# A seven-tap convolution and a SwiGLU feed-forward block on one core: four head-taps change engine in the lead-in, and some words of pair 1's list change place

## The chip, the cores and the metric

The kernel runs on one core of a Trainium2 chip. A core has a matrix engine (TensorE, PE in the profile), a vector engine (VectorE, DVE), a scalar engine (ScalarE, ACT), a general engine (GpSimd, POOL) and an engine that issues DMAs (SyncE, SP). Each works through its own list of instructions in order, and semaphores tie the lists together. The metric is the device time of one execution in microseconds (us). The kernel before took 2473.61, 2478.57 and 2479.82 us in three runs; the median is 2478.57.

## The reference

```python
def _attn_ref(x, weight):                 # x: 8 x 4096 x 192, weight: 8 heads x 7 taps
    w = softmax(weight, axis=-1)          # 7 weights for each head of 24 channels
    x_pad = six rows of zeros in front of each sequence
    out[b, s, h, g] = sum over k of w[h, k] * x_pad[b, s + k, h, g]

def _moe_ref(x, w_gate, w_val, w_out, rms_g):      # x: 32768 x 192 tokens
    xn = x / sqrt(mean(x * x) + 1e-06) * rms_g
    g = xn @ w_gate                       # 192 x 1536
    val = xn @ w_val                      # 192 x 1536
    return (g * sigmoid(g) * val) @ w_out # 1536 x 192
```

The convolution runs along the sequence, one weight for each of 8 heads and 7 taps; its output goes token by token through an RMS norm and a SwiGLU block in float32. The weight matrices come in float64 and are turned into float32 on the chip.

## The kernel before, in words

The 32768 tokens are cut into 32 pairs of 1024 tokens, and a pair into two groups of 512. Pair 0 and pair 1 are special, pairs 2 to 31 repeat one list of words.

Lead-in (pair 0). `conv_first` makes the convolution of pair 0 with the 8 x 7 head-taps shared between two ways. VectorE multiplies and adds the taps `mine`, (1, 3, 5, 6), straight into the tile `y`, one instruction for each head (L418, L422). ScalarE multiplies the others into the tiles `kept` (L404), and TensorE adds them up in the four PSUM banks `ps[0]` to `ps[3]` by multiplying with a unit matrix (L408): four matmuls (one per bank, each recorded as two) for each group of heads. Of the last tap in `mine`, 6, the first `share` = 2 heads also go this second way. Then L428 adds each bank into its part of `y`, in the order 0, 1, 2, 3; after bank 1 and after bank 3, `heat` sends matmuls whose results nobody reads (one after bank 1, three after bank 3), into a second bank of the tile that holds `ps[3]`. `cross` follows: ScalarE squares rows 0 to 5 of `y` (L544; bank c holds rows 2c and 2c+1), VectorE rows 6 and 7 (L551, L554), L558 begins the norm's factors, and TensorE turns `y` round (L589). The weights are converted meanwhile (`convert`, L305 to L345), and `plain` runs pair 0's products (L1091).

Pair 1 has its own hand-written list, `FIRST`; the pairs after it run through `ORDER`. A list is a sequence of words that are emitted in order, and each engine keeps that order among its own instructions. `p3` lets TensorE do three more pieces of the pair's products; `W` advances the preparation of the product weights (`prepare`: L754, L757, L761, L763, L767, L769, then a store to `wd`, L773); other words name an engine (V, A, G, S) and an act. A `+` means the next pair, `++` the one after that, `-` the one before.

The output matmul of a pair is done with seven products instead of eight (a Strassen form). Per chunk j of the hidden features there are four cells a, b, c, d:

- `Aga.j`: ScalarE takes silu of cell a's gate half (L987). `Vma.j`: VectorE multiplies it with the value half into the tile `ht` (L994), which also frees the PSUM tile of that cell for another product (L882 in pair 1, L910 later).
- `Vh1.j`, `Vh3.j`, `Vh2.j`, `Vh4.j`: sums and differences of the four cells, written back in place (L964).
- steps `o1.j` to `o7.j`: TensorE multiplies one of these with a part of the output weights (L937, 12 recorded matmuls in a step). `o7.5` needs `Vh3.5`, `o6.5` needs `Vh2.5`, the steps `o3` need `Vh4`.
- `Ac1`, `As7`, `Ac2`: ScalarE copies of accumulators (L675). `VC21`, `VC22`: VectorE adds them (L1011); `VC21` frees the accumulator tile that the next pair's first product takes, and `VC22` must be done before the steps `o3`, which write the same accumulator.

Words for the pairs ahead: `Vcv5` is tap 5 of the convolution (L445; tap 0 on ScalarE is L441), `Asq`, `Vred`, `Gpow`, `Vbc`, `Gmul` the norm (`Gmul` is POOL's L495), `Spl.i` and `Sft.i` send the tokens out and fetch them back turned, `Sld.i` loads head i of the tokens of a later pair (L154), and `An.g`, `Vd.g`, `Gl.g` or `Vl.g` split operand g of the next pair into the three parts that the products use (`An` L675, `Vd` L820, `Gl` and `Vl` L818). `R` starts the ring: ten loads of prepared weights (L790, 192 KB each) into a tile that the tokens of pair 2 have held until then, so that `R` waits for the last reader of those tokens, `Vd.0`. The products of pair 2 begin with `P5.0` and `P1.0` (L910), the first two words of `ORDER`, ahead of `VC22` and the last six steps `o3` of pair 1.

Of the kernel before, what the change touches and what calls it, by code (L numbers as in the profile page):

```python
# [14 lines left out]
ALU = mybir.AluOpType  # L15
# [5 lines left out]
def kernel(  # L21
# [10 lines left out]
    nc = tc.nc  # L32
# [3 lines left out]
    H, K = weight.shape  # L36
    GS = D // H
# [8 lines left out]
    NJ = PT // P  # L46
# [47 lines left out]
    )  # L94
    FIRST = (
# [14 lines left out]
    )  # L110
    LINE = (
# [56 lines left out]
    def load(p):  # L168
# [34 lines left out]
        out=ps[6][:, 0 : H * K], lhsT=ones[:], rhs=w_row[:], start=True, stop=True,  # L203
# [24 lines left out]
    def load_in(u, q):  # L228
        cols = slice(u * NF * P, (u + 1) * NF * P)
        t = big.tile([P, 2, NF, T], F32, name="ht")  # L230
        t = t[:].rearrange("p a f t -> p (a f t)")[:, 0 : KP * NF * P * 2].bitcast(U32)
        t = raw["in", u] = t.rearrange("p (k n two) -> p k n two", k=KP, two=2)
        if u == 0:
            hold(t[:, :, 0, 0].bitcast(F32))
        for w, rows, turn in ((moe_w_gate, LOW, 0), (moe_w_val, UPP, 1)):
            for k in range(KP):
                at = (k + turn) % KP * HP
                q.dma_start(out=t[rows, k], in_=words(w)[at : at + HP, cols, :])
# [13 lines left out]
    hs = work.tile([P, NP, T], F32, name="hs")  # L252
# [4 lines left out]
    def load_out(i):  # L257
# [19 lines left out]
    taps = cst.tile([P, H, K], F32, name="taps")  # L277
    nc.vector.tensor_reduce(out=stat[:, :, 0], in_=w_sb, axis=AX.X, op=ALU.max)
    nc.vector.tensor_tensor(
        out=taps[:], in0=w_sb, in1=stat[:].to_broadcast([P, H, K]), op=ALU.subtract  # L280
# [7 lines left out]
        out=taps[:], in0=taps[:], in1=ssum[:].to_broadcast([P, H, K]), op=ALU.mult  # L288
# [98 lines left out]

    ys = {}

    def conv_first(mine, share):  # L390

        t = x_sb.pop(0)
        y = ys[0] = yp.tile([P, NJ, D], F32, name="y")
        theirs = [k for k in range(K) if k not in mine]
        two = NJ // 4
        for i, k in enumerate([theirs[0], mine[-1]] + theirs[1:]):
            xk, m = t[:, k : k + NJ, :], next(kept)
            cuts = (0, share) if k in mine else (0, H // 2, H)
            if k == theirs[-1]:
                cuts = (0, H // 2, H // 2 + 2, H)  # L400
            for lo, hi in zip(cuts, cuts[1:]):
                for h in range(lo, hi):
                    hs = slice(h * GS, (h + 1) * GS)
                    nc.scalar.mul(m[:, :, hs], xk[:, :, hs], taps[:, h, k : k + 1])  # L404
                part = slice(lo * GS, hi * GS)
                for c in range(4):
                    to = ps[c][:, 0 : two * D].rearrange("p (j d) -> p j d", d=D)
                    nc.tensor.matmul(  # L408
                        out=to[:, :, part], lhsT=unity, rhs=m[:, c * two : (c + 1) * two, part],
                        start=(i == 0 and lo == 0), stop=True, skip_group_check=True,  # L410
                    )
        for k in mine:
            xk = t[:, k : k + NJ, :]
            for h in range(share if k == mine[-1] else 0, H):
                hs = slice(h * GS, (h + 1) * GS)
                w = taps[:, h, k : k + 1]
                if k == mine[0]:
                    nc.vector.tensor_scalar(  # L418
                        out=y[:, :, hs], in0=xk[:, :, hs], scalar1=w, scalar2=None, op0=ALU.mult
                    )  # L420
                else:
                    nc.vector.scalar_tensor_tensor(  # L422
                        out=y[:, :, hs], in0=xk[:, :, hs], scalar=w, in1=y[:, :, hs],
                        op0=ALU.mult, op1=ALU.add,
                    )
        for c in range(4):
            at = y[:, c * two : (c + 1) * two, :].rearrange("p j d -> p (j d)")
            nc.vector.tensor_tensor(out=at, in0=ps[c][:, 0 : two * D], in1=at, op=ALU.add)  # L428
            if c % 2:
                heat(at, c)  # L430
# [94 lines left out]
    def heat(t, n):  # L525

        for _ in range(n):
            nc.tensor.matmul(  # L528
                out=ps[7][:, 0 : t.shape[1]], lhsT=unity, rhs=t, start=True, stop=True,
                skip_group_check=True,  # L530
            )
# [622 lines left out]
    def done(it):  # L1154
# [21 lines left out]
        out=mask[:], in_=unity.rearrange("p (i h) -> p h i", h=H), axis=AX.X, op=ALU.add  # L1176
    )
    nc.vector.tensor_tensor(
        out=own[:], in0=taps[:].rearrange("p h k -> p k h"),
        in1=mask[:].rearrange("p (o h) -> p o h", o=1).to_broadcast([P, K, H]), op=ALU.mult,  # L1180
# [3 lines left out]
    load_out(0)  # L1184
    load_out(1)
    load_in(1, nc.sync)
    conv_first((1, 3, 5, 6), 2)
    nc.gpsimd.memset(zeros, 0.0)
    nc.sync.dma_start(out=rg_sb[LOW, :], in_=rg)
    nc.sync.dma_start(out=rg_sb[UPP, 0 : KP - 1], in_=rg[:, 1:KP])  # L1190
# [107 lines left out]
```

## Time and profile before

| what | value |
|---|---|
| runs before, us | 2473.61, 2478.57, 2479.82 (median 2478.57) |
| profiled execution: span from the first to the last instruction | 2476.6 us (the page has no other time of it) |
| mean granted TensorE clock | 0.999 of full speed |
| PE busy | 2454.1 us, 99% of the span |
| DVE busy | 2020.8 us, 82% |
| ACT busy | 1018.0 us, 41% |
| POOL busy | 836.2 us, 34% |
| mean DMA traffic | 174 GB/s |

The page belongs to one profiled execution; the three times are other runs. In the rows of the timeline the first number is the start in us from the beginning of the span, the second the length; the bracket at the end tells how long the engine had been idle and which engine and line ended that. A row may gather several instructions in a row of the same kind (x8). In the rows by stretches, the stretch and its length come first, then the busy time of each engine with its count of instructions, then the granted clock (PEclk), the DMA engines' busy share and GB/s. PEld is the loading of weights into the matrix engine.

### The profile page before, as it was taken

Reading aid. Unit: us, or ns where it says so; the run is one execution under the profiler, and the core shown is the slowest. Engines: PE = TensorE matmul, PEld = TensorE weight load, DVE = VectorE, ACT = ScalarE, POOL = GpSimd, SP = SyncE. Lnnn points to the kernel's source line nnn. Section 1 sums busy time; section 2 is a strip of 40 time slices with the busy share of each in tenths; the row PEclk is TensorE's granted clock in tenths of the full one; section 3 lists DMA queues with packets and bytes.
Section 4 is the critical chain, followed back from the end, with each engine's and each line's share of the span. In section 5 each row is a group of like instructions: output and inputs, shape, how many; then the busy total and the mean of one; then the engine's idle time right before and its main releaser. Section 6 shows DMA issues by size and latency. Waiting matters only on the chain.

```text
span 2476.6 us, 69229 instructions
## 1 busy us (share of the span) xinstructions
PE 2454.1 (99%) x29152; PEld 1896.0 (77%) x29152; DVE 2020.8 (82%) x2526; ACT 1018.0 (41%) x1435; POOL 836.2 (34%) x624
## 2 busy tenths in 40 slices
PE   8999999999999999999999999999999999999999
PEld 5546777877777877777787778777777877778777
DVE  8687888888888888888888887888888888888864
ACT  6443344434344334344334444343444343443332
POOL 0541333333333333334233434333433333333322
PEclk9999999999999999999999999999999999999999
DMA  7363677666687666786666777666776666876653
GB/s 151 60 205 107 171 200 194 190 161 175 173 205 185 189 162 173 176 211 178 177 167 171 191 193 191 173 167 172 199 198 187 160 172 172 205 185 192 159 162 94
DMA packets 716392, 430.55 MB, mean 174 GB/s; under 512 B 510330, under 2 KB 702386, under 8 KB 716082
## 3 DMA queue, kind: packets, MB, share of 16 engines
q1 hardware_dynamic: 712336, 425.21, 66.4%
q8 instruction: 230, 3.77, 0.7%
q10 hardware_dynamic: 3746, 0.92, 0.2%
q14 instruction: 80, 0.66, 0.1%
HBM read 366.96 MB, written 58.98 MB: 172 GB/s over the span
## 4 chain that ended last, share of the span: by engine, by line
PE 92%; DVE 4%; DMA 2%; issue 1%; ACT 1%; POOL 0%; SPq 0%; DVEq 0%; POOLq 0%; ACTq 0%
PE ps L910 54%; PE ps L937 35%; PE ps L882 2%; DMA xb<-xd 1%; DMA ring<-wd 1%; DVE y L445 0%; DVE ht L1109 0%; PE ps L408 0%; DVE ht L994 0%; DVE ps L981 0%; PE ps L528 0%; DVE part L345 0%; DVE part L330 0%; DVE ht L964 0%; ACT part L675 0%
## 5 line engine op out<-in xcount | busy, mean ns | idle before, releaser
L910 PE MATMUL ps<-part,ring 64*128 64x512 f32 x12240 | 1419.9, 389 | 3.4 <-DMA ring<-wd 2.3
L910 PEld LDWEIGHTS ps<-part,ring 64*128 64x128 f32 x12240 | 1151.3, 184 | 258.4 <-DVE ps L981 12.0
L987 ACT ACTIVATE tt<-ps 128x512 f32<-128x512 f32 x744 | 439.3, 599 | 714.5 <-PE ps L910 661.2
L994 DVE TENSOR_TENSOR ht<-ps,tt 128x512 f32<-128x512 f32 x744 | 497.7, 686 | 254.8 <-ACT tt L987 252.3
L937 PE MATMUL ps<-ht,wo_sb 128*32 128x384 f32 (+2 forms) x7272 | 468.3, 380 | 1.9 <-DVE tt L1011 1.1
L964 POOL TENSOR_TENSOR ht<-ht 128x512 f32<-128x512 f32 x180 | 273.6, 1527 | 541.6 <-PE ps L937 534.1
L937 PE MATMUL ps<-ht,x 128*32 128x384 f32 (+2 forms) x6696 | 440.3, 380 | 2.9 <-DVE ht L964 2.9
L937 PEld LDWEIGHTS ps<-ht,wo_sb 128*32 128x32 f32 x7272 | 325.0, 110 | 115.8 <-issue 14.8
L937 PEld LDWEIGHTS ps<-ht,x 128*32 128x32 f32 x6696 | 300.3, 110 | 93.0 <-DVE ht L964 3.1
L981 DVE TENSOR_TENSOR ps<-ps,tt 128x1024 f32<-128x1024 f32 x240 | 295.8, 1233 | 52.6 <-ACT tt L675 23.0
L445 DVE SCALAR_TENSOR_TENSOR y<-xh,tp,y 128x1536 f32<-128x1536 f32 x186 | 336.5, 1809 | 0.2
L675 ACT COPY ps<-ps 128x1024 f32<-128x1024 f32 (+1 forms) x151 | 134.6, 892 | 402.8 <-PE ps L910 326.1
L675 ACT COPY tt<-ps 128x384 f32<-128x384 f32 (+1 forms) x182 | 151.7, 834 | 225.0 <-PE ps L937 161.0
L964 POOL TENSOR_TENSOR hs<-ht 128x512 f32<-128x512 f32 x120 | 155.4, 1295 | 262.0 <-DVE ht L994 262.0
L474 POOL TENSOR_SCALAR r<-r 128x8 f32<-128x8 f32 x31 | 6.2, 199 | 509.8 <-DVE r L469 509.7
L937 PE MATMUL ps<-hs,x 128*32 128x128 f32 (+2 forms) x2232 | 161.2, 379 | 0.0
L964 DVE TENSOR_TENSOR ht<-ht 128x512 f32<-128x512 f32 x192 | 132.7, 705 | 21.3 <-PE ps L937 18.3
L937 PEld LDWEIGHTS ps<-hs,x 128*32 128x32 f32 x2232 | 106.8, 110 | 29.7
L964 DVE TENSOR_TENSOR ht<-hs,ht 128x512 f32<-128x512 f32 x156 | 112.2, 766 | 11.0 <-PE ps L937 10.2
L820 DVE SCALAR_TENSOR_TENSOR part<-part,xb 128x1024 fp32r<-128x1024 f32 x87 | 120.1, 1380 | 0.0
L818 POOL TENSOR_TENSOR part<-xb,part 128x1024 fp32r<-128x1024 f32 x29 | 69.6, 2401 | 122.3 <-PE ps L910 86.1
L495 POOL TENSOR_TENSOR xh<-y,s 128x1536 f32<-128x1536 f32 x30 | 89.9, 2997 | 15.3 <-DVE s L487 7.7
(132 smaller groups left out, 1421.1 us busy)
## 6 DMA issues: line engine op xcount, KB each, us to landing
ring<-wd SPq DMA_DIRECT2D x1440, 192.0 KB
xb<-xd SPq DMA_DIRECT2D x60, 512.0 KB
xd<-xh SPq DMA_DIRECT2D x240, 96.0 KB
xh<-in_x_dram SPq DMA_DIRECT2D x192, 105.0 KB
xb<-xd SPq DMA_DIRECT2D x60, 256.0 KB
out_dram<-o_sb SPq DMA_DIRECT2D x126, 96.0 KB
out_dram<-o_sb SPq DMA_DIRECT2D x62, 128.0 KB
wd<-part SPq DMA_DIRECT2D x5, 1152.0 KB
```

The costliest lines, as they stand in the source:

```text
L445: nc.vector.scalar_tensor_tensor(out=y, in0=xk, scalar=w, in1=y, op0=ALU.mult, op1=ALU.add)
L495: e.tensor_tensor(out=yn[p].rearrange("p a t -> p t a"), in0=y, in1=ss[:].rearrange("p (t o) -> p t o", o=1).to_broadcast([P, TB, GS]), op ...
L675: nc.scalar.copy(out=dst, in_=src)
L818: e.tensor_tensor(out=split_of(g, 1).bitcast(F32R), in0=src, in1=high, op=ALU.subtract)
L820: nc.vector.scalar_tensor_tensor(out=split_of(g, 2).bitcast(F32R), in0=high, scalar=1.0 + SPLIT, in1=src, op0=ALU.mult, op1=ALU.subtract,)
L882: nc.tensor.matmul(out=self.both(j, c)[:, h, :], lhsT=wf[HALF[h], k, 2 * HOME[j] + f, :], rhs=rb[HALF[h], k, g, :], start=(k == 0), stop=( ...
L910: nc.tensor.matmul(out=self.both(j, c)[:, h, :], lhsT=left[HALF[h]], rhs=right[HALF[h]], start=(first and q == 0), stop=True, skip_group_c ...
L937: nc.tensor.matmul(out=self.acc(b)[i * Q : (i + 1) * Q, at : at + n], lhsT=left, rhs=cols, start=fresh, stop=True, skip_group_check=True, ...
L964: engine[eng].tensor_tensor(out=dst, in0=a, in1=b, op=op)
L981: nc.vector.tensor_tensor(out=self.both(j, c), in0=self.both(j, "b"), in1=s5, op=ALU.add)
L987: nc.scalar.activation(out=tt[:, t, :], in_=self.both(j, c)[:, 0, :], func=AF.Silu)
L994: nc.vector.tensor_tensor(out=self.hv(j, "abcd".index(c)), in0=self.both(j, c)[:, 1, :], in1=tt[:, t, :], op=ALU.mult,)
```

## The change

In `conv_first` the argument `share` goes from 2 to 0, and a new argument `give` is 2. The two head-taps of tap 6 and the last two heads of the last other tap (4) no longer pass through ScalarE and TensorE but are four more instructions of VectorE. TensorE has six groups of matmuls instead of eight. The banks are added in the order 0, 3, 1, 2, so that the three matmuls of `heat` after bank 3 now come ahead of the one after bank 1.

In `FIRST`, `Vh2.0` moves behind `Vma.1`. The five words that split operands 0 and 4 of pair 2 (`An.0 An.4 Gl.0 Vd.0 Vl.4`) move behind `Vh2.5`, so that `Vh1.5`, `Vh3.5` and `Vh2.5` stand ahead of them on VectorE, `Ac1` ahead of `An.0` on ScalarE, and `R`, which waits for `Vd.0`, behind them. The token loads `Sld.5`, `Sld.6` and `Sld.7` of pair 3 move ahead of `R`, tap 0 of pair 3 (`Acv0`) ahead of `As7`, and taps 1 and 2 (`Vcv1`, `Vcv2`) ahead of `Vh4.3`, where before they stood around `VC21` and `Vh4.4`. The pieces `p` are the same in number. `ORDER` is unchanged.

```diff
 FIRST = (
-    "Vmc.0 W p1 Gpow+ W W W p1 W p1 Agd.0 W p1 Vmd.0 Vbc+ Vh1.0 p1 Gmul+ p1 Vh3.0 W Vh2.0",
-    "p1 Aga.1 W W W Vma.1 p1 W W p1 Spl.0+ p1 Agb.1 Vmb.1 Spl.1+ p1 Spl.2+ W p1 Spl.3+ W",
+    "Vmc.0 W p1 Gpow+ W W W p1 W p1 Agd.0 W p1 Vmd.0 Vbc+ Vh1.0 p1 Gmul+ p1 Vh3.0 W",
+    "p1 Aga.1 W W W Vma.1 Vh2.0 p1 W W p1 Spl.0+ p1 Agb.1 Vmb.1 Spl.1+ p1 Spl.2+ W p1 Spl.3+ W",
...
-    "p1 Vmd.5 An.0+ Gl.0+ Vd.0+ An.4+ Vl.4+ p1 Vh1.5 p2 Ac1 Sld.3++ Vh3.5 Vh2.5 p3",
-    "Sld.4++ p1 Vh4.5 p1 Vh4.0 R p1 As7 p1 Sld.5++ p2 Sld.6++ p1 Sld.7++ p2 Ac2 p1 Vh4.3",
-    "p9 Vh4.2 Acv0++ p2 Vh4.1 p1 Vcv1++ p1 VC21 p1 Vh4.4 Vcv2++",
+    "p1 Vmd.5 p1 Vh1.5 p2 Ac1 Sld.3++ Vh3.5 Vh2.5 An.0+ An.4+ Gl.0+ Vd.0+ Vl.4+ p3 Sld.4++",
+    "Sld.5++ Sld.6++ Sld.7++ p1 Vh4.5 p1 Vh4.0 R Acv0++ p1 As7 p4 p2 Ac2 p1 Vcv1++ Vcv2++ Vh4.3",
+    "p9 Vh4.2 p2 Vh4.1 p2 VC21 p1 Vh4.4",
 )
...
-def conv_first(mine, share):
+def conv_first(mine, share, give):
...
     for i, k in enumerate([theirs[0], mine[-1]] + theirs[1:]):
         xk, m = t[:, k : k + NJ, :], next(kept)
+        if k in mine and not share:
+            continue
         cuts = (0, share) if k in mine else (0, H // 2, H)
         if k == theirs[-1]:
-            cuts = (0, H // 2, H // 2 + 2, H)
+            cuts = (0, H // 2, H - give)
...
-    for c in range(4):
+    for h in range(H - give, H):
+        k, hs = theirs[-1], slice(h * GS, (h + 1) * GS)
+        nc.vector.scalar_tensor_tensor(
+            out=y[:, :, hs], in0=t[:, k : k + NJ, hs], scalar=taps[:, h, k : k + 1],
+            in1=y[:, :, hs], op0=ALU.mult, op1=ALU.add,
+        )
+    for c in (0, 3, 1, 2):
...
-conv_first((1, 3, 5, 6), 2)
+conv_first((1, 3, 5, 6), 0, 2)
```

## The prediction

> **What bounds the kernel now.** I read the page first, then busy time by stretches, PE's waits, and the timeline of the stretches that the change touches (a row there: start and length in us, engine, line, operation, output<-inputs, count, and in brackets the idle time before it and what ended it).
>
> ```profile
> span 2476.6 us, 69229 instructions
> ...
> core 0: us, PE busy (x) PEld busy (x) DVE busy (x) ACT busy (x) POOL busy (x), PEclk, DMA share, GB/s
> 41.00:92.70 51.70, 51.70 (x244) 23.15 (x244) 48.66 (x66) 34.28 (x55) 11.14 (x11) 1.00 0.25 51
> ...
> 199.40:205.20 5.80, 2.96 (x28) 2.06 (x32) 4.74 (x7) 0.48 (x1) 0.00 (x0) 0.71 0.70 221
> ...
> 143.50:145.50 2.00, 0.81 (x4) 0.00 (x0) 2.00 (x3) 0.13 (x1) 1.04 (x1) 1.00 1.02 369
> ...
> 230.00:1350.00 1120.00, 1118.27 (x13654) 883.93 (x13652) 934.53 (x1137) 462.72 (x629) 391.46 (x285) 1.00 0.70 182
> ```
>
> From 230 us on, PE (TensorE) is busy 1118.27 of 1120 us: the repeated pairs are bound by PE, and the change does not touch their list. So whatever PE gains before 230 us comes off the end, one for one. The losses sit earlier: in the lead-in before PE runs without a break (41 to 92.7 us), and in pair 1. In 199.4 to 205.2 us PE worked 2.96 of 5.8 us, and its mean clock was 0.71, that is (1 - 0.71) x 5.8 / 0.5 = 3.4 us at half speed.
>
> The sum is made against the profiled span, 2476.6 us. The median of the three runs is 2478.57, 2.0 above it (they span 2473.61 to 2479.82); gains are subtracted from the median. 0.3% of it, 7.4 us, is about what a measurement of this kernel can tell from no change.
>
> **Part 1, the lead-in.**
>
> ```profile
> 10.92 9.32 PE L408 MATMUL ps<-part 128*128 128x192 f32 x64
> ...
> 13.50:14.36 0.86, 0.86 (x10) 0.86 (x9) 1.00 0.98 207
> ...
> 8.61 7.32 DVE L422 SCALAR_TENSOR_TENSOR y<-x,taps,y 128x192 f32<-128x192 f32 x22
> ...
> 8.57 9.10 ACT L404 ACTIVATE part<-x,taps 128x192 f32<-128x192 f32 x26
> ...
> 19.61 1.49 DVE L428 TENSOR_TENSOR y<-ps,y 128x384 f32<-128x384 f32 x3 [3.67 <-PE ps L408]
> ...
> 21.63 0.56 DVE L428 TENSOR_TENSOR y<-ps,y 128x384 f32<-128x384 f32 x1 [0.54 <-PE ps L528]
> ...
> 20.20 0.36 ACT L544 ACTIVATE sq<-y 128x192 f32<-128x192 f32 x1 [1.02 <-DVE y L428]
> ...
> 22.90 0.19 ACT L544 ACTIVATION_READ_ACCUMULATOR sq<-y 128x1 f32 x1
> ...
> 23.55 0.17 DVE L558 TENSOR_SCALAR ss<-ss 128x8 f32<-128x8 f32 x1
> ```
>
> The 64 matmuls of L408 follow each other without a gap, and DVE (VectorE) waits 3.67 us for them. The second row (busy time of L408 in one stretch) is one group for two heads: 8 matmuls, 0.86 us. The change drops two of the three such groups, so PE is done 1.75 us earlier and the first bank sum starts at 17.86 instead of 19.61. ACT (ScalarE) makes 22 head-taps instead of 26, done by 8.57 + 22 x 0.35 = 16.27, ahead of PE. DVE makes 4 more: 4 x 0.333 = 1.33 us, from 15.93 to 17.26, inside the wait, with 0.6 us to spare. If that cover were gone, each further head-tap would cost 0.33 us.
>
> Bank order 0, 3, 1, 2: the sum of bank 3 no longer waits 0.54 us for the warm-up matmuls of L528 that write the same tile. But banks 1 and 2 come later, and six ACT squares read banks 0, 1 and 2 at 0.49 us each. The new order gives: sums from 17.86, 18.52 (bank 3's last matmul comes 0.6 us after bank 0's), 19.0 and 19.45; squares of bank 0 from 18.45, of bank 1 from 19.58, four in a row to 21.53; L558 at 21.57. Before it was 23.55, so the lead-in gains 1.98. Without any gain from the order it would be 1.75. Everything from there to 100 us is a chain of compute; nothing there waits for a transfer, and I carry the 1.98 through.
>
> **Part 2, the word Vh2.0 behind Vma.1 (pair 1, about 142 us).**
>
> ```profile
> 141.21 3.32 POOL L495 TENSOR_TENSOR xh<-y,s 128x1536 f32<-128x1536 f32 x1
> ...
> 139.62 2.18 DVE L964 TENSOR_TENSOR ht<-ht 128x512 f32<-128x512 f32 x1
> ...
> 141.91 3.09 DVE L964 TENSOR_TENSOR ht<-hs,ht 128x512 f32<-128x512 f32 x1
> ...
> 144.92 0.41 DVE L757 TENSOR_SCALAR part<-part 128x512 uint32<-128x512 uint32 x1
> ...
> 145.26 0.68 DVE L994 TENSOR_TENSOR ht<-ps,tt 128x512 f32<-128x512 f32 x1
> ...
> 145.99 2.85 PE L882 MATMUL ps<-xb,part 64*128 64x512 f32 x12 [1.68 <-DVE ht L994]
> ...
> 156.48 0.68 DVE L994 TENSOR_TENSOR ht<-ps,tt 128x512 f32<-128x512 f32 x1
> ...
> 149.55 10.57 PE L882 MATMUL ps<-xb,part 64*128 64x512 f32 x48
> ...
> 95.08 1.01 POOL L337 TENSOR_TENSOR wo_sb<-part 128x384 f32<-128x384 f32 x1
> ...
> 95.14 1.17 DVE L313 TENSOR_SCALAR part<-hs 128x384 uint32<-128x384 uint32 x1
> ```
>
> PE stands 1.68 us, from 144.31, until Vma.1 (L994, 145.26) frees a bank. Ahead of Vma.1 on DVE stand Vh2.0 (3.09 us instead of some 0.7, because POOL's scaling L495 runs until 144.53) and L757. It looks like 1.68 us to win. But now L757 comes straight behind Vh3.0, while POOL's L495, issued at 141.21, is already waiting for Vh3.0 to end at 141.80. The last two rows show what then happens: a DVE tensor_scalar of the same kind, issued 0.06 us behind a POOL operation, took 1.17 us and ended 0.22 after it. So L757 ends near 144.9 either way; Vma.1 follows at 144.82, PE at 145.55: 0.44 us earlier. And Vh2.0, now behind Vma.1, pushes the weight chain (L763 and what follows) some 0.17 back; the fourth product of the next round (149.55 + 3/4 x 10.57 = 157.48) waits for the L994 that ends at 157.16, a slack of 0.3. Little of the 0.44 survives: I take 0.1. [...]
>
> [...]
>
> **Part 3, the end of pair 1 (about 195 to 226 us).**
>
> ```profile
> 195.28 0.84 PE L937 MATMUL ps<-ht,wo_sb 128*32 128x384 f32 x12
> ...
> 194.58 1.04 ACT L675 CAST part<-ring 128x1024 fp32r<-128x1024 f32 x1
> ...
> 195.70 2.94 POOL L818 TENSOR_TENSOR part<-ring,part 128x1024 fp32r<-128x1024 f32 x1 [9.25 <-ACT part L675]
> ...
> 196.31 0.68 DVE L994 TENSOR_TENSOR ht<-ps,tt 128x512 f32<-128x512 f32 x1
> ...
> 196.91 2.81 DVE L820 SCALAR_TENSOR_TENSOR part<-part,ring 128x1024 fp32r<-128x1024 f32 x1
> ...
> 200.78 0.68 DVE L964 TENSOR_TENSOR hs<-ht 128x512 f32<-128x512 f32 x1
> ...
> 201.49 0.69 DVE L964 TENSOR_TENSOR ht<-ht 128x512 f32<-128x512 f32 x1
> ...
> 202.24 6.21 PE L937 MATMUL ps<-ht,x 128*32 128x384 f32 x84 [2.86 <-DVE ht L964]
> ...
> 180.19 4.46 SPq L154 DMA_DIRECT2D xh<-in_x_dram  x5
> ...
> 199.79 4.61 SPq L790 DMA_DIRECT2D ring<-wd  x10
> ...
> 211.03 1.58 ACT L441 ACTIVATE y<-xh,tp 128x1536 f32<-128x1536 f32 x1 [2.02 <-DMA xh<-in_x_dram]
> ...
> 216.91 1.81 DVE L445 SCALAR_TENSOR_TENSOR y<-xh,tp,y 128x1536 f32<-128x1536 f32 x1
> ...
> 218.64 0.55 DVE L1011 TENSOR_TENSOR tt<-ps,tt 128x384 f32<-128x384 f32 x1
> ...
> 219.24 1.65 PE L910 MATMUL ps<-part,ring 64*128 64x512 f32 x12 [0.39 <-DVE tt L1011]
> ...
> 222.04 4.11 PE L937 MATMUL ps<-ht,wo_sb 128*32 128x384 f32 x72 [1.14 <-DVE tt L1011]
> ```
>
> PE's step o7.5 (the row at 202.24; a step is 12 matmuls and 0.645 us, as in the 4.11 us for 72 of the last row with their tail) waits 2.86 us for Vh3.5 (201.49). Then half clock costs about 1.5 us more: half of the 3.0 us in which PE worked in that stretch. Ahead of Vh3.5 stand Vd.0 (2.81, again behind POOL's Gl.0) and Vl.4. Now Vh1.5 follows Vmd.5 (196.31 + 0.68) at 197.03, and Vh3.5 is ready 0.71 us later, at 197.75 (the spacing of the two L964). Gl.0 needs An.0, and An.0 now follows Ac1, which needs the step at 195.28, done at 196.12: Ac1 at 196.23, An.0 (1.04 us) from 196.61 to 197.65, Gl.0 at 197.72. A margin of 0.03 us, so either may come first. If Gl.0 does (2.3 us of port), Vh3.5 ends at 200.65 and o7.5 starts at 200.70; if Vh3.5 does, Vh2.5 is the late one, and o6.5, two steps on, starts at 201.4. P5.0, 23 steps after the start of o7.5 or 21 after that of o6.5, has its turn at 215.5 or 214.95 (it ran at 219.24). The wait shrinks from 2.86 to some 1.3 or 0.9 us, below the 1.68 us of part 2, where the clock stayed at 1.00 (the row from 143.50).
>
> Next, the taps Vcv1 and Vcv2 (1.81 each) leave their places ahead of the two L1011 and run near 206 us, where DVE idles. Then P5.0 is no longer held by the first L1011. The second comes behind Vh4.4 (0.6), which needs the last step before P5.0 (0.3 after its end): 215.5 + 0.3 + 0.6 + 0.55 = 216.95, or 216.4, and that is when the step of 222.04 starts. Gain at that row: 5.0 or 5.6; with Gl.0 first a little likelier, I take 5.2. After it PE was continuous. What is late next: Vd.0 ends near 202.6 and with it the ring's ten loads start 2.9 us later than 199.79; they took 4.6 us to issue, and P5.0 needs the first at 215, so this is hidden by some 8 us. The three token loads of SP that landed for ACT at 211.03 now issue behind the five at 180.19, near 185 us, ahead of the ring. Acv0 (1.58 us) now sits on ACT ahead of As7, which must be done (0.5 us) before the eighth step after o7.5, at 205.9: it costs nothing while the loads land before 203.7. [...]
>
> [...]
>
> **Sum.** 1.98 + 0.1 + 5.2 = 7.3 us: 2478.57 - 7.3 = 2471.3.
>
> **The rivals.** [...] Second, one part does not carry: the clock drop belonged to this profile alone, or the lead-in's 2 us are lost at a later wait; gain 5.3 to 5.8, time about 2473. Third, no effect: PE's waits only move, 2478. [...]
>
> **How the numbers follow.** The forecast as worked has 0.48, and its scatter lies about half on either side of 7.4 us; the first rival 0.26, the second 0.09, the third 0.05, the slower one 0.12. Faster: 0.24 + 0.26 = 0.50; within 0.3%: 0.24 + 0.09 + 0.05 = 0.38; slower: 0.12. The range runs from 2466.5 (the best case and 2 us of scatter between runs) to 2477 (the third rival nearly), leaving the slower case out.
>
> **What would show it.** L558 near 21.6 us; the PE wait at 144 us at 1.2 or less; no stretch below clock 1 near 200 us; the PE wait there at most 1.6; both waits for L1011 gone; the 230 us row's busy share unchanged. A wait of ACT for xh ahead of As7, or of PE for the ring, would make it wrong.

## The result, and the profile after

The changed kernel takes 2470.19 us (median; 2469.40 to 2473.39), the kernel before, run beside it, 2475.85 us (2473.61 to 2479.82). The ratio is 0.9977, with a 95% interval of 0.9967 to 0.9987: faster by 5.7 us, which is less than the 0.3% that the prediction called measurable, but no change at all lies outside the interval. The forecast was 2471.3 us, 7.3 below the 2478.57 of the first three runs.

The profiled execution of the changed kernel has a span of 2471.6 us; its own time, 2473.39, is the longest of its runs. Lines from `conv_first` on have numbers 2 to 8 higher than before: L558 is L566, L757 is L765, L937 is L945, L964 is L972, L994 is L1002, L1011 is L1019. First the page:

```profile
span 2471.6 us, 69198 instructions
...
PE 2452.5 (99%) x29136; PEld 1894.3 (77%) x29136; DVE 2024.1 (82%) x2530; ACT 1016.2 (41%) x1431; POOL 833.3 (34%) x624
```

Busy time by two of the stretches that the prediction shows, with the same columns:

```profile
199.40:205.20 5.80, 5.80 (x114) 4.68 (x110) 5.76 (x7) 0.96 (x2) 0.00 (x0) 1.00 0.52 143
...
230.00:1350.00 1120.00, 1118.73 (x13642) 886.30 (x13642) 933.89 (x1136) 461.48 (x628) 389.50 (x285) 1.00 0.70 181
```

PE's waits between 100 and 230 us (engine, tile and line that waited, what it waited for, us in total, times, longest):

```profile
PE ps L890 <- DVE ht L1002: 1.4, 2, 1.2
PE ps L945 <- DVE ht L972: 1.3, 1, 1.3
```

The half clock near 200 us is gone (1.00 instead of 0.71, PE busy for the whole 5.8 us; what is left of the wait there, 1.3 us, now ends ahead of this stretch), the repeated pairs are as before (1118.73 busy us of 1120, before 1118.27), and of the waits of pair 1 those for L1019 no longer appear. A further wait of PE, for L337, ends at 100.19 us before (0.80 us) and at 98.38 after (0.81 us); the change does not touch it. Now the timeline of the places that the change touches; the columns are as in the prediction.

```profile
7.48 1.69 DVE L420 TENSOR_SCALAR y<-x,taps 128x192 f32<-128x192 f32 x7 [2.21 <-DMA x<-in_x_dram]
...
10.66 7.96 PE L410 MATMUL ps<-part 128*128 128x192 f32 x48 [0.33 <-ACT part L406]
...
17.22 0.74 DVE L430 SCALAR_TENSOR_TENSOR y<-x,taps,y 128x192 f32<-128x192 f32 x2
...
18.07 2.08 DVE L436 TENSOR_TENSOR y<-ps,y 128x384 f32<-128x384 f32 x4
...
21.72 0.17 DVE L566 TENSOR_SCALAR ss<-ss 128x8 f32<-128x8 f32 x1 [0.53 <-ACT sq L552]
...
23.52 0.49 PE L597 MATMUL ps<-part,y 128*128 128x128 f32 x2 [1.41 <-ACT part L590]
...
139.42 3.31 POOL L503 TENSOR_TENSOR xh<-y,s 128x1536 f32<-128x1536 f32 x1
...
139.93 3.08 DVE L765 TENSOR_SCALAR part<-part 128x512 uint32<-128x512 uint32 x1
...
142.93 0.67 DVE L1002 TENSOR_TENSOR ht<-ps,tt 128x512 f32<-128x512 f32 x1
...
143.66 2.85 PE L890 MATMUL ps<-xb,part 64*128 64x512 f32 x12 [1.15 <-DVE ht L1002]
...
155.48 2.85 PE L890 MATMUL ps<-xb,part 64*128 64x512 f32 x12 [0.26 <-DVE ht L1002]
...
195.97 2.37 POOL L826 TENSOR_TENSOR part<-ring,part 128x1024 fp32r<-128x1024 f32 x1 [11.27 <-ACT part L683]
...
196.01 2.88 DVE L972 TENSOR_TENSOR ht<-ht 128x512 f32<-128x512 f32 x1
...
198.95 4.76 PE L945 MATMUL ps<-ht,x 128*32 128x384 f32 x84 [1.31 <-DVE ht L972]
...
214.03 1.67 PE L918 MATMUL ps<-part,ring 64*128 64x512 f32 x12
...
215.64 4.11 PE L945 MATMUL ps<-ht,wo_sb 128*32 128x384 f32 x72
```

The lead-in ends (L566) at 21.72 instead of 23.55 although its tokens landed 0.7 us later in this execution. The wait at 144 us fell from 1.68 to 1.15, and 0.26 of a new wait stands one round on, at 155.48. The step o7.5 (the row at 198.95) waits 1.31 instead of 2.86, behind Vh3.5, which was issued 0.04 us after POOL's Gl.0 (L826) and took 2.88 us. P5.0 (214.03) and the six steps behind it (215.64) start without a wait.

For the account I cut the span at two places that every run has: the first matmul of the turn that follows the lead-in (25.35 before, 23.52 after), and the start of the group of 72 matmuls ahead of the ring products (222.04, 215.64), called "the 72" from here. The stretch between them took 196.69 us before and 192.12 after. For the lead-in I count from the first L418 (the landing of x) to L558, because that landing alone varies from 6.66 to 7.48 us between runs.

### The profile page after: what moved, and what is told of

Read it like the earlier page. It is cut to its first block, busy times and chain, and to the rows that moved or that the text cites. A ratio compares the mean times of both kernels' runs of the same rounds, so it can differ in the third digit from the quotient of the medians.

```text
span 2471.6 us, 69198 instructions
## 1 busy us (share of the span) xinstructions
PE 2452.5 (99%) x29136; PEld 1894.3 (77%) x29136; DVE 2024.1 (82%) x2530; ACT 1016.2 (41%) x1431; POOL 833.3 (34%) x624
## 4 chain that ended last, share of the span: by engine, by line
PE 90%; DVE 3%; DMA 3%; SPq 1%; issue 1%; POOL 1%; ACT 1%; DVEq 0%; POOLq 0%; ACTq 0%
PE ps L918 55%; PE ps L945 35%; DMA xb<-xd 1%; DMA ht<-in_moe_w_val_dram 1%; DMA ring<-wd 1%; SPq L154 0%; DVE ht L972 0%; POOL part L775 0%; SPq L238 0%; DVE ht L1117 0%; DVE ht L1002 0%; DVE part L771 0%; DVE y L453 0%; DMA x<-in_x_dram 0%; DVE ps L989 0%
## 5 line engine op out<-in xcount | busy, mean ns | idle before, releaser
L1002 DVE TENSOR_TENSOR ht<-ps,tt 128x512 f32<-128x512 f32 x744 | 498.0, 686 | 254.3 <-ACT tt L995 252.2
L945 PE MATMUL ps<-ht,wo_sb 128*32 128x384 f32 (+2 forms) x7272 | 468.3, 380 | 0.8 <-POOL wo_sb L337 0.8
L972 POOL TENSOR_TENSOR ht<-ht 128x512 f32<-128x512 f32 x180 | 272.2, 1520 | 543.9 <-PE ps L945 536.4
L945 PE MATMUL ps<-ht,x 128*32 128x256 f32 (+2 forms) x6696 | 439.1, 379 | 1.3 <-DVE ht L972 1.3
L945 PEld LDWEIGHTS ps<-ht,wo_sb 128*32 128x32 f32 x7272 | 325.1, 110 | 114.5 <-issue 14.5
L945 PEld LDWEIGHTS ps<-ht,x 128*32 128x32 f32 x6696 | 299.6, 110 | 90.9 <-DVE ht L972 1.6
L972 POOL TENSOR_TENSOR hs<-ht 128x512 f32<-128x512 f32 x120 | 155.0, 1292 | 262.6 <-DVE ht L1002 262.6
L945 PE MATMUL ps<-hs,x 128*32 128x128 f32 (+2 forms) x2232 | 161.4, 379 | 0.0
L972 DVE TENSOR_TENSOR ht<-ht 128x512 f32<-128x512 f32 x192 | 135.0, 717 | 15.2 <-PE ps L945 12.6
L945 PEld LDWEIGHTS ps<-hs,x 128*32 128x32 f32 x2232 | 106.9, 110 | 29.6
L828 DVE SCALAR_TENSOR_TENSOR part<-part,xb 128x1024 fp32r<-128x1024 f32 x87 | 120.1, 1381 | 0.0
L972 DVE TENSOR_TENSOR ht<-hs,ht 128x512 f32<-128x512 f32 x156 | 109.2, 747 | 11.3 <-PE ps L945 10.7
L826 POOL TENSOR_TENSOR part<-xb,part 128x1024 fp32r<-128x1024 f32 x29 | 69.7, 2403 | 124.0 <-PE ps L918 82.1
```

What stands on the lines that cost most here:

```text
L826: e.tensor_tensor(out=split_of(g, 1).bitcast(F32R), in0=src, in1=high, op=ALU.subtract)
L828: nc.vector.scalar_tensor_tensor(out=split_of(g, 2).bitcast(F32R), in0=high, scalar=1.0 + SPLIT, in1=src, op0=ALU.mult, op1=ALU.subtract,)
L945: nc.tensor.matmul(out=self.acc(b)[i * Q : (i + 1) * Q, at : at + n], lhsT=left, rhs=cols, start=fresh, stop=True, skip_group_check=True, ...
L972: engine[eng].tensor_tensor(out=dst, in0=a, in1=b, op=op)
L1002: nc.vector.tensor_tensor(out=self.hv(j, "abcd".index(c)), in0=self.both(j, c)[:, 1, :], in1=tt[:, t, :], op=ALU.mult,)
```

## The experiments

Each ran with the kernel before beside it; the interval of a median difference is 2 to 3 us to either side. So the profiles of single stages carry the verdicts, and the medians only confirm their sum. In the table, 144 us and 155 us are the two places at which PE waits for Vma.1 and Vma.2 (L994, after the change L1002).

| run | what is in it | turn to the 72, us | PE's wait: 144 us / 155 us / o7.5 / P5.0 / the 72 | median against before, us |
|---|---|---|---|---|
| before | | 196.69 | 1.68 / 0 / 2.86 / 0.39 / 1.14 | |
| lead-in alone | part 1 | 196.67 | 1.69 / 0 / 2.86 / 0.40 / 1.13 | -2.1 |
| Vh2.0 alone | part 2 | 196.98 | 1.16 / 0.26 / 2.84 / 0.39 / 1.14 | +0.9 |
| end of pair 1 alone | part 3 | 192.05 | 1.68 / 0 / 1.32 / 0 / 0 | -4.2 |
| after, again | all | 192.15 | 1.15 / 0.26 / 1.33 / 0 / 0 | -5.4 |
| split alone | part 3, five words | 197.55 | 1.69 / 0 / 1.31 / 4.16 / 0 | +2.3 |
| split and loads | part 3 but the taps | 193.74 | 1.69 / 0 / 1.31 / 0.39 / 1.14 | -3.8 |
| taps and loads | part 3 but the split | 195.32 | 1.69 / 0 / 2.87 / 0 / 0 | 0.0 |
| both orders | all, and two more swaps | 190.04 | 0 / 0.86 / 0 / 0 / 0 | -8.6 |
| two more rounds | all, the two swaps, and the same order in two more rounds | 189.24 | 0 / 0 / 0 / 0 / 0 | -9.2 |

**The lead-in alone.** The changed `conv_first`, with `FIRST` as before.

```diff
-    conv_first((1, 3, 5, 6), 2)
+    conv_first((1, 3, 5, 6), 0, 2)
```

> The lead-in's part alone (four head-taps to VectorE, bank order 0, 3, 1, 2), the list of pair 1 as before. My theory (the gain is the sum of local waits of TensorE, carried to the end): the first sum of the norm's factors about 1.8 to 2.0 us earlier than 23.55, the wait near 200 us still 2.9 us, the first of the last six steps o3 of pair 1 at 220.1 to 220.3 instead of 222.04, and the time 2 us less (0.1%). [...] Rival (the lead-in's gain is lost again before pair 1 ends): o3 at 222.

The time was 2473.15 against 2475.29 us, ratio 0.9992 (0.9983 to 1.0001). L558 comes 14.17 us after the first L418 (21.11 - 6.94), against 16.78 in the profile before and 16.10 to 16.53 in five other runs with the old lead-in; behind the turn everything is as before (196.67). To split the gain, one run keeps the taps' move but adds the banks in the old order, one has the new order alone. Each of the two was executed only once (2475.99 and 2477.15 us), so only their profiles are read:

```diff
-        for c in (0, 3, 1, 2):
+        for c in range(4):
```

> The kernel before with the four head-taps moved to VectorE, but the sums of the lead-in in the old order 0, 1, 2, 3. Theory (the taps' move gives about 1.65 us at the first sum, the new order 0.3 us between the first sum and L558): the first sum starts as early after x has landed as in the lead-in run, and from there to L558 it takes 3.9 us as in the kernel before, against 3.6 to 3.7 with the new order; the sum of bank 3 waits some 0.5 us for the warm-up matmuls. Rival (the order is worth nothing, ScalarE's squares set the end): 3.6 to 3.7. Second rival (the order is worth more once PE is early): 4.2 or more.

```diff
-        for c in range(4):
+        for c in (0, 3, 1, 2):
```

> The kernel before with nothing changed but the order of the lead-in's sums, 0, 3, 1, 2; the four head-taps stay on TensorE. Theory: the first sum starts as late as in the kernel before (VectorE waits some 3 us for TensorE), from there to L558 it takes 3.6 to 3.7 us instead of 3.94. Rival (without the taps' move bank 3 is not ready in time, and its sum now stands ahead of banks 1 and 2): 4.0 us or more.

VectorE's timeline, first with the taps moved and the old order:

```profile
7.16 1.93 DVE L420 TENSOR_SCALAR y<-x,taps 128x192 f32<-128x192 f32 x8 [1.89 <-DMA x<-in_x_dram]
...
17.75 1.49 DVE L436 TENSOR_TENSOR y<-ps,y 128x384 f32<-128x384 f32 x3
...
19.78 0.56 DVE L436 TENSOR_TENSOR y<-ps,y 128x384 f32<-128x384 f32 x1 [0.54 <-PE ps L536]
...
21.62 0.17 DVE L566 TENSOR_SCALAR ss<-ss 128x8 f32<-128x8 f32 x1
```

And with the new order alone:

```profile
7.13 1.93 DVE L418 TENSOR_SCALAR y<-x,taps 128x192 f32<-128x192 f32 x8 [1.87 <-DMA x<-in_x_dram]
...
19.22 2.16 DVE L428 TENSOR_TENSOR y<-ps,y 128x384 f32<-128x384 f32 x4 [2.92 <-PE ps L408]
...
22.96 0.17 DVE L558 TENSOR_SCALAR ss<-ss 128x8 f32<-128x8 f32 x1 [0.53 <-ACT sq L544]
```

The taps put the first sum 10.59 us behind the landing (17.75 - 7.16) instead of 12.09 (19.22 - 7.13); the old order takes 3.87 us from there to L558, the new one 3.74, and 3.58 in the lead-in run. With the old order the sum of bank 3 waits 0.54 us for the warm-up matmuls of `heat`; with the new one that wait is gone, and instead the last square of ScalarE sets the end (the 0.53 us in front of L558). So between these two profiles the taps are worth 1.5 us up to the first sum, and the order 0.1 to 0.3 behind it. The 1.5 is a low value: with the old taps the first sum stood 12.09 to 12.84 us behind the landing in seven profiles, with the new ones 10.58 to 10.86 in six, on the mean 1.7 us earlier.

**Vh2.0 alone.** Only this pair of lines of `FIRST` is changed.

```diff
-    "... p1 Gmul+ p1 Vh3.0 W Vh2.0",
-    "p1 Aga.1 W W W Vma.1 p1 W W ...",
+    "... p1 Gmul+ p1 Vh3.0 W",
+    "p1 Aga.1 W W W Vma.1 Vh2.0 p1 W W ...",
```

> Vh2.0 behind Vma.1 alone. My theory (the tensor_scalar L757 stands behind POOL's scaling either way): L757 takes about 3.1 us in the place of Vh2.0, the wait of TensorE near 144 us falls from 1.68 to about 1.2, a wait of about 0.3 comes up twelve us later, and o3 starts within 0.2 us of 222.04; time as before. Rival (Vh2.0 alone had held Vma.1): no wait at 144 us, o3 at 220.4 to 221.3, time 0.7 to 1.7 us less.

2476.16 against 2475.29 us, ratio 1.0005 (0.9996 to 1.0013). The wait at 144 us falls by 0.5, 0.26 of it returns at 155 us, and o7.5 starts 176.95 us after the turn, against 176.89 before: worth nothing. The longer stretch to the 72 (196.98) I put down to where the half clock falls, below.

**The end of pair 1 alone.** The last three lines of `FIRST` as changed, all else as before.

```diff
-    "... Vmd.5 An.0+ Gl.0+ Vd.0+ An.4+ Vl.4+ p1 Vh1.5 ... Vh3.5 Vh2.5 p3",
+    "... Vmd.5 p1 Vh1.5 ... Vh3.5 Vh2.5 An.0+ An.4+ Gl.0+ Vd.0+ Vl.4+ p3 Sld.4++",
...
-    "... R p1 As7 p1 Sld.5++ p2 Sld.6++ p1 Sld.7++ p2 Ac2 p1 Vh4.3",
-    "p9 Vh4.2 Acv0++ p2 Vh4.1 p1 Vcv1++ p1 VC21 p1 Vh4.4 Vcv2++",
+    "Sld.5++ Sld.6++ Sld.7++ ... R Acv0++ p1 As7 p4 p2 Ac2 p1 Vcv1++ Vcv2++ Vh4.3",
+    "p9 Vh4.2 p2 Vh4.1 p2 VC21 p1 Vh4.4",
```

> The end of pair 1 alone (split words behind Vh2.5, token loads ahead of the ring, three taps earlier). My theory: the wait for Vh3.5 falls from 2.86 to about 1.3 us, no half clock, no wait for L1011; o3 at about 217.4 instead of 222.04, so 4.6 us, and all of it reaches the end, with a scatter of 1 to 2 us from the landings of the ring's loads in the repeated pairs; time about 4.6 us less (0.19%). Rival (the repeated pairs run slower in the new phase): o3 as said, but 1 to 2 us given back after 230 us, steadily pair by pair, time about 3 us less.

2471.12 against 2475.29 us, ratio 0.9984 (0.9975 to 0.9992). The stretch is 4.64 us shorter, the half clock is gone, and o7.5 waits 1.32. This is the largest part, and smaller than the 5.2 forecast. Three runs take it apart. The first moves the five split words alone:

```diff
-    "p1 Vmd.5 An.0+ Gl.0+ Vd.0+ An.4+ Vl.4+ p1 Vh1.5 p2 Ac1 Sld.3++ Vh3.5 Vh2.5 p3",
+    "p1 Vmd.5 p1 Vh1.5 p2 Ac1 Sld.3++ Vh3.5 Vh2.5 An.0+ An.4+ Gl.0+ Vd.0+ Vl.4+ p3",
```

> The kernel before, with only the five words of the weight split (An.0, Gl.0, Vd.0, An.4, Vl.4) moved behind Vh2.5; token loads and taps keep their old places, and nothing else is changed. Theory (the wait at o7.5 and the taps are two separate costs, about 2.1 and 2.5 us of the 4.6 found in the end-of-pair run): PE's wait at o7.5 is 1.3 us instead of 2.86 and no stretch shows half clock; P5.0 and the step after it still wait for the two L1011, since Vcv1 and Vcv2 stay in front of them. Because the ring's loads issue later while the three last token loads stay behind them, Acv0 gets its rows later than 211.0. From the start of the first turn to the last six steps ahead of the ring products: 194.5 us instead of 196.7; time 2.1 us under the kernel before. Rival (the taps are the whole cost, the split words only shift the wait): no gain, 196.7. Second rival (the later token loads hold the taps back until they delay P5.0 more than before): 196 or more.

2477.77 against 2475.47 us, ratio 1.0007 (0.9998 to 1.0017). The stretch did not shrink to 194.5 us but grew to 197.55: my theory fell and the second rival (196 or more) holds. Rows of its timeline:

```profile
200.58 4.76 PE L937 MATMUL ps<-ht,x 128*32 128x384 f32 x84 [1.30 <-DVE ht L964]
...
202.52 5.40 SPq L790 DMA_DIRECT2D ring<-wd  x10
...
207.97 5.56 SPq L154 DMA_DIRECT2D xh<-in_x_dram  x3
...
215.95 1.57 ACT L441 ACTIVATE y<-xh,tp 128x1536 f32<-128x1536 f32 x1 [10.07 <-DMA xh<-in_x_dram]
...
217.56 1.82 DVE L445 SCALAR_TENSOR_TENSOR y<-xh,tp,y 128x1536 f32<-128x1536 f32 x1 [3.68 <-ACT y L441]
...
219.90 2.93 PE L910 MATMUL ps<-part,ring 64*128 64x512 f32 x12 [4.16 <-DVE tt L1011]
...
222.76 5.39 PE L937 MATMUL ps<-ht,wo_sb 128*32 128x384 f32 x72
```

The gain at o7.5 comes as in the whole part (1.30 us of wait, no half clock). But the ring's loads now start at 202.52 instead of 199.79, and the three token loads that still stand behind them on SP's queue issue at 207.97. ScalarE's tap waits for them until 215.95, the tap of VectorE behind it until 217.56, L1011 behind that, and P5.0 stands for 4.16 us. Behind that idle time the clock stands at 0.50 again (218.59 to 225.42): the 12 matmuls of P5.0 take 2.93 instead of 1.65 us and the 72 take 5.39 instead of 4.11. The sum of these terms up to the end of the 72 is -1.55 (wait) - 1.45 (84 matmuls in 4.76 instead of 6.21) - 1.53 (both L1011 waits) + 4.16 + 2 x 1.28 = +2.2 us; the median says +2.3.

The second moves the token loads too, and leaves only the taps in their old places (the diff is against the run of the whole part):

```diff
-    "Sld.5++ Sld.6++ Sld.7++ p1 Vh4.5 p1 Vh4.0 R Acv0++ p1 As7 p4 p2 Ac2 p1 Vcv1++ Vcv2++ Vh4.3",
-    "p9 Vh4.2 p2 Vh4.1 p2 VC21 p1 Vh4.4",
+    "Sld.5++ Sld.6++ Sld.7++ p1 Vh4.5 p1 Vh4.0 R p1 As7 p4 p2 Ac2 p1 Vh4.3",
+    "p9 Vh4.2 Acv0++ p2 Vh4.1 p1 Vcv1++ p1 VC21 p1 Vh4.4 Vcv2++",
```

> The kernel before, with the five split words behind Vh2.5 and the three last token loads ahead of the ring; Acv0, Vcv1 and Vcv2 keep their old places. It differs from the split-only run in the loads alone, and from the end-of-pair run in the taps' places alone. Theory (the split move pays only with its cover: its 4.2 us wait ahead of P5.0 came from token rows queued behind the ring): o7.5 waits 1.3 us, no half clock, the tap of ScalarE does not wait for a transfer, and what stays is what the taps' places cost, about 0.4 us ahead of P5.0 and 1.1 ahead of the next step. From the first turn to the last six steps 193.6 us (192.05 + 1.5), time 3.1 us under the kernel before. Rival (the taps' places are what delays P5.0 in the split-only run, whatever the loads do): P5.0 waits 2 us or more again and the stretch is 195.5 or longer.

2472.81 against 2476.60 us, ratio 0.9988 (0.9979 to 0.9998). PE's waits from 190 to 240 us:

```profile
PE ps L937 <- DVE ht L964: 1.3, 1, 1.3
PE ps L937 <- DVE tt L1011: 1.1, 1, 1.1
PE ps L910 <- DVE tt L1011: 0.4, 1, 0.4
```

And the tap of ScalarE in the timeline:

```profile
205.45 1.58 ACT L441 ACTIVATE y<-xh,tp 128x1536 f32<-128x1536 f32 x1
```

The three loads ahead of the ring are the whole difference between a loss of 2 us and a gain of 3: with them the tap waits for no transfer and runs at 205.45. What the taps' old places cost is 1.1 + 0.4, and the stretch is 193.74 (193.6 expected).

The third has loads and taps in their new places and the split words in the old ones, against the kernel before:

```diff
-    "... Vh3.5 Vh2.5 p3",
-    "Sld.4++ p1 Vh4.5 p1 Vh4.0 R p1 As7 p1 Sld.5++ p2 Sld.6++ p1 Sld.7++ p2 Ac2 p1 Vh4.3",
-    "p9 Vh4.2 Acv0++ p2 Vh4.1 p1 Vcv1++ p1 VC21 p1 Vh4.4 Vcv2++",
+    "... Vh3.5 Vh2.5 p3 Sld.4++",
+    "Sld.5++ Sld.6++ Sld.7++ p1 Vh4.5 p1 Vh4.0 R Acv0++ p1 As7 p4 p2 Ac2 p1 Vcv1++ Vcv2++ Vh4.3",
+    "p9 Vh4.2 p2 Vh4.1 p2 VC21 p1 Vh4.4",
```

> The kernel before, with only the token loads issued ahead of the ring and Acv0, Vcv1, Vcv2 in their new earlier places; the five words of the weight split stay ahead of Vh1.5, and nothing else is changed. Theory (two separate costs): the wait at o7.5 stays at 2.8 us and the clock halves there as before; both waits for L1011 ahead of P5.0 and of the step after it (0.39 and 1.14 us) are gone; from the start of the first turn to the last six steps 195.0 us instead of 196.7, time 1.6 us under the kernel before. Rival (one cost: the taps were late only because o7.5 was): no gain, 196.7. Second rival: the half clock falls away without the wait shrinking, 193.5.

2475.48 against 2475.47 us, ratio 0.9999 (0.9990 to 1.0008). In its profile the stretch is 1.37 shorter (195.32), both L1011 waits are gone, and o7.5 still waits 2.87 with half clock behind it. The theory holds in the profile; the median shows nothing of the 1.4, which is inside its interval.

**The changed kernel again.** No edit.

> The changed kernel once more, nothing altered. The parts measured up to the last six steps add up to 6.5 us (1.9 + 0.0 + 4.6), while its first runs were 5.7 below the kernel before, and its profile spent 2255.9 us on the rest against 2251 to 2254.5 in the five others. Theory (that difference is the scatter of single executions, from ring loads that land a little late in the repeated pairs): the rest takes 2251 to 2254 us this time, and the time is about 6 us under the kernel before. Rival (the change itself gives about 1 us back in the repeated pairs): 2255.5 to 2256.5 us again, and 5 us or less under the kernel before.

2470.08 against 2475.47 us, ratio 0.9979 (0.9970 to 0.9988). The stretch is 192.15 again, and the rest behind the 72 took 2253.33 us instead of 2255.93; in the nine other runs named so far it lies between 2251.0 and 2255.3. PE's waits behind 230 us, in the profile after, tell a good part of this:

```profile
PE ps L918 <- DMA ring<-wd: 1.9, 5, 0.8
```

The same row gave 2.3 us in the profile before, 0.6 in this run, 0.2 with the end of pair 1 alone: ring loads that land a little late at changing places of the repeated pairs. So the profile speaks for scatter. The median (-5.4, after -5.7 the first time) stays 1 us short of the 6.6 that the parts add up to, between what theory and rival said; that remainder lies inside the interval, and what it is stays open.

**Both orders.** The changed kernel with two swaps that take away what the two remaining waits wait for: Vma.1 ahead of the three weight steps, and An.4 ahead of An.0.

```diff
-    "p1 Aga.1 W W W Vma.1 Vh2.0 p1 W W ...",
+    "p1 Aga.1 Vma.1 W W W Vh2.0 p1 W W ...",
...
-    "... Vh3.5 Vh2.5 An.0+ An.4+ Gl.0+ Vd.0+ Vl.4+ p3 Sld.4++",
+    "... Vh3.5 Vh2.5 An.4+ An.0+ Gl.0+ Vd.0+ Vl.4+ p3 Sld.4++",
```

> The changed kernel with two further moves: Vma.1 ahead of the three W (so ahead of L757), and An.4 ahead of An.0 (so that Gl.0 is ready only when Vh3.5 and Vh2.5 are through). [...]

2466.65 against 2475.29 us, ratio 0.9968 (0.9955 to 0.9980). Rows of its timeline, at 140 us and at the end of the pair:

```profile
138.88 3.33 POOL L503 TENSOR_TENSOR xh<-y,s 128x1536 f32<-128x1536 f32 x1
...
140.31 0.69 DVE L1002 TENSOR_TENSOR ht<-ps,tt 128x512 f32<-128x512 f32 x1 [0.85 <-ACT tt L995]
...
140.92 1.57 DVE L765 TENSOR_SCALAR part<-part 128x512 uint32<-128x512 uint32 x1
...
154.36 1.99 PE L890 MATMUL ps<-xb,part 64*128 64x512 f32 x8 [0.86 <-DVE ht L1002]
...
195.68 0.69 DVE L972 TENSOR_TENSOR ht<-hs,ht 128x512 f32<-128x512 f32 x1
...
195.80 2.81 POOL L826 TENSOR_TENSOR part<-ring,part 128x1024 fp32r<-128x1024 f32 x1 [12.22 <-ACT part L683]
...
196.29 3.41 DVE L828 SCALAR_TENSOR_TENSOR part<-part,ring 128x1024 fp32r<-128x1024 f32 x1
```

Vma.1 (L1002) took its usual 0.69 us in the middle of POOL's 3.33, and L765, now behind it, 1.57. The 1.15 us wait is gone, and 0.86 of wait appears one round later, so this swap gains 0.5 from the turn to the matmuls at 154.36. At the end of the pair POOL's Gl.0 now comes 0.12 us after the last Vh issued, o7.5 does not wait at all, and the long instruction is now L828 (3.41 us instead of the 1.22 it took after the change), which nothing on PE needs soon: another 1.5 us. Both waits fall by a change of order alone, with VectorE's work the same. The stretch is 2.1 us shorter than after the change (190.04 against 192.12). The medians point the same way (-8.6 against -5.4 and -5.7 us), but their intervals overlap.

**Two more rounds.** The kernel of the last run, with the same order in the next two rounds.

```diff
-    "... W Vh3.1 W Vh2.1 p1 Aga.2 Vma.2 p2 W p1 Agb.2 ...",
-    "... W Vh1.2 p2 Vh3.2 Vh2.2 p1 Aga.3 W Vma.3 p1 W",
+    "... W Vh3.1 W p1 Aga.2 Vma.2 Vh2.1 p2 W p1 Agb.2 ...",
+    "... W Vh1.2 p2 Vh3.2 p1 Aga.3 Vma.3 W Vh2.2 p1 W",
```

> The kernel of the both-orders run (the changed kernel with Vma.1 ahead of the three weight steps and An.4 ahead of An.0), and now the same order in the next two rounds too: Vh2.1 behind Vma.2, Vma.3 ahead of the weight step that stood before it, and Vh2.2 behind that. Nothing else is changed. Theory (the 0.86 us wait in the second round is again Vma.2 standing behind a scaling that the GpSimd operation stretches): that wait falls to 0.3 us or less, and the time is 0.5 to 0.9 us below the both-orders run, about 9.3 us under the kernel before. Rival (the wait there is set by the weight chain, not by the order): 0.86 stays, no gain. Second rival (the scaling now stands in the way of the third round): another wait of 0.5 us or more appears near 166 us, no gain or a loss.

2466.28 against 2475.47 us, ratio 0.9964 (0.9952 to 0.9977). In the last run Vh2.1 (L972 at 152.13) had taken 1.57 us ahead of Vma.2, next to an instruction of POOL (L775, 151.51, 1.64 us); now Vma.2 comes first and takes 0.69. The 0.86 us at 155 is gone and no wait above 0.2 us is left on PE between 100 and 230 us; the stretch is 0.80 shorter than in the last run. The median is 0.4 below it, which the intervals can't tell apart; the profile's stage shows the theory right.

## Why the prediction was right, and where it was wrong

**The bound** held: PE behind 230 us is as busy as before, and every stage gain before it shows in the end as far as the medians can tell. From the stages the parts add up to 2.0 + 0 + 4.6 = 6.6 us against 7.3 forecast; the medians gave 5.7 and 5.4. Part of why 2470.19 came so near to 2471.3 is luck: the median I subtracted from, 2478.57 of three runs, was 2.7 above that of eight.

**Part 1** was 1.98 and is 2.0 when counted from the landing of x (14.33 us to L558 as the mean of five runs with the new lead-in, 16.32 over six with the old one). One step of it was off, the 0.6 us that VectorE was to have to spare. The row at 17.22 shows its two last taps ending at 17.96, and the first sum follows at 18.07 with no wait; so it is in five of the six profiles with the taps moved. VectorE's taps took what I had worked out (10.5 us from landing to end). TensorE came early: in the profile before, its matmuls had begun late, behind 28 warm-up matmuls that ended at 11.08 us there and at 9.78 in the Vh2.0 run. In the profile before these start 0.21 us apart up to 10.70 us and 0.11 from there on, in the profile after 0.21 up to 8.99 and 0.11 from 9.16 on; the trace's record of full clock begins at 10.68 and at 9.10. So that moment differed by 1.58 us between these two executions. How much cover is left differs too: in the second profile of the changed kernel VectorE waited 0.33 us for TensorE. So the cover is mostly used up, and in most executions a further head-tap would cost about its 0.33 us, which no run tried. The order brought 0.1 to 0.3, as the 0.2 said.

**Part 2** was 0.1 and is 0.1 or nothing: from the turn to the matmuls at 155 us, 131.96 instead of 132.03. It went as forecast: POOL's scaling was issued at 139.42, L765 0.51 us later, and L765 then took 3.08 us (0.41 before). The 0.44 came as 0.53. But the matmuls at 155.48 need the end of Vma.2, and that came 131.90 us after the turn, 0.09 later than before (131.81), behind the pushed weight chain. Before, those matmuls had started 0.22 us after that end, so little more than 0.1 could be won there; the rest of the earlier start is lost again in the new wait of 0.26.

**Part 3** is the term that was mis-sized: 5.2 forecast, 4.6 measured. The 2.3 us of port that the forecast gave to Gl.0 is a term that no run shows; what the profile after shows in its place is Gl.0 at 2.37 us and Vh3.5, issued 0.04 us behind it, at 2.88 instead of 0.69. The times of the steps held one by one: Gl.0 came 0.04 us ahead of Vh3.5 (0.03 forecast), the wait is 1.31 (1.3), the clock stays at 1.00, both L1011 waits are gone, the ring waits for nothing. Of the 5.2, 5.0 was for this case and 0.2 for the mix with the other order. What failed is the walk from o7.5 to the 72. I counted steps (23 to P5.0, then 0.3 + 0.6 + 0.55) and got 16.25 us; it takes 16.69, 15.08 of it up to P5.0 (14.8 by the count). The last leg, 1.45 us by the sum, takes 1.61, because P5.0's own 12 matmuls set it (1.65 us already in the old row at 219.24), not L1011. The old rows held that figure: 219.24 - 202.24 = 17.00, less 1.45 for the half clock and 0.39 of wait, is 15.16. Summing the time that goes, 1.55 of wait, 1.45 of half clock, 0.39 and 1.14 of wait, gives 4.5, the right size. The step "token loads ahead of the ring: costs nothing" was right, and the split-alone run shows what its cover was worth: without it the part loses 2 us.

**The rivals.** The better order did not come by itself: L765 was issued 0.51 us behind POOL's scaling, Vh3.5 0.04 us behind Gl.0. But the two runs with other orders show what it is worth: o7.5 without a wait 1.5 us more, and Vma.1 gains at 144 us by standing ahead of L765, not by L765 being issued ahead of the scaling. The best case behind the lower end of the range (2466.5) is shown by no run of the changed kernel: both of its profiles have the waits of 1.15 and 1.3 us. The second rival falls: the clock drop belonged to no single profile, the run with the new order alone, with a wait of 2.86 us, shows it too (0.50 from 202.99 on), and in the taps-and-loads run, with 2.87, the 84 matmuls behind the wait take 6.44 us (6.21 before, 4.76 after). No effect and the slower case fall too: PE is busy for 1118.73 of 1120 us in the repeated pairs, 1118.27 before.

## What to carry to other kernels

Size a removed stall by the waits and slow matmuls that go, each from its own row, and check the sum against the old walk between two landmarks; counting steps by a mean duration, with a last leg priced too short, lost 0.4 us here. Where an instruction of VectorE takes several times its usual length next to one of GpSimd (here 2.88 us instead of 0.69, issued 0.04 us behind it), look at which of the two is issued first, and let the long one fall behind the short one that PE waits for: here moving one word gained 0.5 us at one place and 1.5 at another, and three more words 0.8. When a word moves back on a queue, look at everything issued behind it: the same five words lost 2 us or gained 3, depending on three loads on SyncE's queue.

## What the runs showed of the hardware

**The clock dropped behind 2.11 us of idle time.** In pair 1 of the kernel before, half speed lasted 3.41 us, from 201.83 to 205.24. Busy time by stretches of this length, with the columns of the stretches above: first the kernel before, the stretch with the 1.68 us wait at 144 us (counted back from the drop in steps of this length), the one ahead of the drop and the one at half speed.

```profile
143.80:147.21 3.41, 1.73 (x10) 0.69 (x8) 3.41 (x6) 0.00 (x0) 1.33 (x2) 1.00 1.03 313
198.42:201.83 3.41, 0.96 (x20) 0.49 (x12) 3.38 (x4) 0.00 (x0) 0.22 (x1) 1.00 0.26 77
201.83:205.24 3.41, 3.00 (x29) 2.06 (x32) 2.34 (x4) 0.48 (x1) 0.00 (x0) 0.50 0.95 303
```

The run with the new order alone, the stretch with the 2.86 us wait of o7.5 and the two behind it:

```profile
199.58:202.99 3.41, 1.30 (x24) 1.08 (x28) 3.17 (x5) 0.35 (x1) 0.00 (x0) 1.00 0.67 182
202.99:206.40 3.41, 3.41 (x38) 2.48 (x34) 0.84 (x2) 0.14 (x1) 0.00 (x0) 0.50 0.96 337
206.40:209.81 3.41, 3.41 (x70) 2.72 (x63) 0.69 (x1) 0.48 (x1) 0.00 (x0) 1.00 0.81 128
```

The split-alone run, around its wait of 4.16 us at P5.0:

```profile
215.18:218.59 3.41, 0.55 (x12) 0.18 (x4) 1.03 (x1) 1.57 (x1) 0.00 (x0) 1.00 0.02 3
218.59:222.00 3.41, 2.10 (x10) 1.73 (x12) 3.41 (x4) 0.00 (x0) 0.00 (x0) 0.50 0.00 0
222.00:225.42 3.42, 3.42 (x32) 2.08 (x34) 3.42 (x10) 1.02 (x2) 0.00 (x0) 0.50 0.39 118
```

Behind the stretch with 1.73 busy us of 3.41 the clock stayed at 1.00; behind those with 1.30 (2.11 us idle), 0.96 and 0.55 it stood at 0.50. At half speed, a stretch with 2.10 busy us was followed by another one at 0.50, though at full speed 1.73 had gone with 1.00. Counted in steps of this length from the beginning of the record of full clock (10.68 and 9.10 us) to 2450 us, the profiles before and after have one stretch that half speed followed, the one with 0.96; the least busy of the others have 1.73 and 2.10 us. Between 1.30 and 1.73 these rows have no case. When the half speed began also set its price: in the kernel before it began at 201.83, 0.41 us ahead of o7.5, so that PE worked 3.00 us of it, in the run with the new order alone at 202.99, with o7.5 under way since 201.69, so that PE worked all 3.41. The second costs (3.41 - 3.00) / 2 = 0.2 us more by an estimate from these rows, which is what the Vh2.0 run took more from o7.5 to the 72 with the same waits (20.03 against 19.80).

**Hundredths went with 2.2 us.** Gl.0 at 195.97 and Vh3.5 at 196.01: the later one took 2.88 instead of 0.69 us. In all five profiles with this order of words PE then waited 1.30 to 1.33 us, so nothing shows that the two changed places between executions. Where Gl.0 came 0.12 us after the last Vh instead (both orders), that Vh took its 0.69.
